# Three more attention units with V as the stationary operand of PV and key sums on Pool, and a later slot for the second norm

## The chip, the cores and the metric

The kernel runs on one core of a Trainium2 chip. A core has engines with instruction queues of their own: TensorE (PE) for matmuls, with a weight load (PEld) ahead of each; VectorE (DVE); ScalarE (ACT); GpSimd (POOL); and SyncE (SP), which here issues the DMA transfers. They wait for each other through semaphores. On-chip memory is SBUF; PE writes its results to banks of PSUM. The metric is the time of one execution in microseconds on the device, the median of the runs shown.

## The reference: what is computed

A transformer block on x of 2048 rows and 512 columns, in bf16. A modulation vector of six parts (sa, ca, ga, sb, cb, gb) is made from `c` and `w_mod`. Then

```python
h = layernorm(x) * (1 + ca) + sa
x = x + ga * attention(h)      # 32 query heads, 8 kv heads, head size 128, 2048 cached keys
h = layernorm(x) * (1 + cb) + sb
x = x + gb * gated_mlp(h)      # w_in, gelu, a 2048 x 2048 mixing matrix w_sp, w_out
```

Attention projects h with `wq`, takes softmax(q k^T / sqrt(128)) v for each head and projects with `wo`. Of the output of attention, four query heads share one kv head. The MLP normalises half of its hidden part and mixes it over the rows with `w_sp`.

## The kernel before

**Units.** Attention is cut into 128 units (`NU`). Unit u is kv group g = u // 16 (`HKV` = 8 groups) and query tile j = u % 16 of 128 rows (`NT` = 16), with the four query heads of that group (`REP`). A loop over iterations `it` from 0 to `NU + 5` starts the scores of unit `it`; each iteration has eight slots (`NSLOT`). In each slot the program writes, in this order: what was put off to that slot with `at(it, slot, fn)`; a part of the scores of unit `it` (`qk`, two or so 128 x 512 matmuls into a double bank of PSUM and one exp on ACT); a part of PV of an earlier unit (`pv_part`); a part of the q projection for later units (`fill`, L959); and one matmul of the output projection `wo` of a still earlier unit (L1209). The order on each engine is the order in which the program writes the instructions; nothing reorders them, so a waiting instruction holds up all behind it on its engine. PV of a unit comes one to three iterations after its scores (`pv_at`), its output projection three iterations after that (`wo_at`). PE's work in a steady iteration is 16 matmuls of scores, 16 or 64 of PV, 4 of `wo` and 4 of q.

**Three kinds of units.**
- *Row units* (`by_rows`; two of every three from unit 5 to 121, `TURN_A` to `TURN_B`) have queries on the partitions. The exp sums its row on the way (`accum_out`, L1033). The probabilities P are then transposed by a DMA that SP issues, one for each head (`turn_rows`, L1116), and DVE makes 1/sum from the row sums (L1120, L1123).
- *Sums units* (`by_sums`; every third one, 7, 10, ... up to 109) have keys on the partitions, so that P needs no transposing (L1063 for the scores, L1070 for the exp). Their row sums come from `key_sums`: Pool adds the 16 key tiles of P (15 adds, L1085), SP transposes the result (`xn<-onorm`, L1100), and two iterations and more later DVE reduces and inverts it (`close`, L1104, L1105).
- *Old column units* (the rest: 0 to 4, and 112, 115, 118 and 121 to 127) also have keys on the partitions, but take their sums from a column of ones beside V.

**PV.** Row and sums units use `pv_rows`: V is the stationary operand and P moves through, 16 matmuls of 512 columns (L1131) into one bank, whose result DVE casts to `oT` (L1140). The output projection then gets a bank for each head (`each` in `wo_proj`), and DVE scales each with 1/sum and adds it to `xacc` (L1202, four a unit). Old column units use `pv`: P is the stationary operand and V with the column of ones moves, 64 matmuls of 129 columns (L1152); DVE takes the reciprocal of the sums and scales (L1163, L1164, twice a unit), SP transposes (`oT<-onorm`, L1175), and the projection's four heads add up in one bank, which DVE adds to `xacc` once (L1196; in the first group it copies it, L1194).

**Where P lives.** The tile for a unit's P is one of three (`homes`: `pT0`, `pT1`, `wsp`), given out in turn as their last users are done. The transposes of a row unit therefore wait for all readers of the unit that had the tile before, and these are PV and, for a sums unit, Pool's adds.

**Start and end.** In the first iterations PE also waits for the first layernorm, in pieces: DVE normalises (L687), SP transposes, and DVE applies the modulation to the transposed tiles `hT` (L806, in `ln1_mod`), which the q projections read. In the last group (units 112 to 127) each output projection ends a query tile: x is updated (for tiles 0 to 11 by Pool, L1225 and L1226), and `ln2` does the second layernorm in three steps: `first` has the statistics on DVE (L698, L699) and 1/std on Pool (L679, L683); `second` normalises on DVE (L687) and has SP transpose the tile (`acc<-acc`, L1248); `third` applies the modulation on DVE (L1255). They are put in slots of the iterations after the projection. The MLP follows (L1436 to L1645), of which some is mixed into the last iterations. A fallback after it runs only if a softmax sum lies outside a safe range.

The slots of Pool's adds and of the second norm are set by these lines:

```python
for kt in range(1, NKT):
    at(*divmod(u * NSLOT + kt // 2 + 1, NSLOT), lambda kt=kt: add(kt))
...
at(it + 1, 0 if j >= NT - CT else 2, first)
at(it + 1, 4, second)
at(it + 2, 3, third)
```

`NKT` is 16 and `CT` is 4.

Of the kernel before, what the change touches and what calls it, by code (L numbers as in the profile page):

```python
# [575 lines left out]
def kernel(  # L576
# [21 lines left out]
    _, HKV, SK, DH = A_k_cache.shape  # L598
# [6 lines left out]
    NT = S // P  # L605
# [4 lines left out]
    CT = 512 // P  # L610
    FC = _f_chunk(FH)
    NFHC = FH // FC
    NSLOT = NKT // 2
# [62 lines left out]
    def rstd_of(mv, n, tag):  # L676

        ve = stat.tile([P, CT], FP32, name=f"ve_{tag}")
        nc.gpsimd.tensor_scalar(  # L679
            out=ve[:, :n], in0=mv[:, :, 1], scalar1=LN_EPS, scalar2=None, op0=ALU.add  # L680
        )
        rstd = stat.tile([P, CT], FP32, name=f"rstd_{tag}", bufs=4)
        nc.gpsimd.tensor_tensor(out=rstd[:, :n], in0=ve[:, :n], in1=mhalf[:, :n], op=ALU.pow)  # L683
        return rstd

    def normalise(dst, src, mv, rstd):
        nc.vector.tensor_scalar(  # L687
            out=dst,
            in0=src,
            scalar1=mv,  # L690
            scalar2=rstd,
            op0=ALU.subtract,
            op1=ALU.mult,
        )

    def ln_stats(mv, j, src):
        st = stat.tile([P, 1, nc.vector.BN_STATS_DIM], FP32, name="bnst")
        nc.vector.bn_stats(out=st[:, 0, :], in_=src)  # L698
        nc.vector.bn_aggr(out=mv[:, j, :], in_=st[:])  # L699
# [87 lines left out]
    def ln1_stats(j0, n):  # L787
        for j in range(j0, j0 + n):
            ln_stats(mv1, j, x_sb[:, j, :])
        return rstd_of(mv1[:, j0 : j0 + n, :], n, "ln1")  # L790
# [153 lines left out]
    first = {1: ln1_stats(1, 1)}  # L944
# [33 lines left out]
    TURN_A, TURN_B = CT + 1, NU - 6  # L978
# [3 lines left out]
    def by_rows(u):  # L982
        return TURN_A <= u < TURN_B and (u - TURN_A) % len(LAGS) < len(LAGS) - 1

    def by_sums(u):
        return TURN_A <= u < (HKV - 1) * NT and not by_rows(u)

    row_units = [u for u in range(NU) if by_rows(u)]

# [16 lines left out]
    def at(it, slot, fn):  # L1006
        later.setdefault((it, slot), []).append(fn)

    def qk(u, i):
        g, j = divmod(u, NT)  # L1010
        b, jj = g * NCH + j // CT, j % CT
        if i == 0:
            if homes[u] == "wsp":
                pTs[u] = wspp.tile([P, NT, 512], BF16, name="wsp")
            else:
                pTs[u] = late.tile([P, NKT, 512], BF16, name=homes[u], bufs=1)
            if by_rows(u):
                rsums[u] = stat.tile([P, NSLOT], FP32, name="rs")
            if by_sums(u):
                key_sums(u)  # L1020
# [56 lines left out]
    def key_sums(u):  # L1077
        acc = res.tile([P, D], FP32, name="acc", bufs=2)
        sums = late.tile([P, REP, DH], BF16, name="onorm", bufs=3)[:].rearrange(
            "p r q -> p (r q)"  # L1080
        )
        pT = pTs[u]

        def add(kt):
            nc.gpsimd.tensor_tensor(  # L1085
                out=acc[:] if kt < NKT - 1 else sums,
                in0=pT[:, 0, :] if kt == 1 else acc[:],
                in1=pT[:, kt, :],
                op=ALU.add,
            )  # L1090

        for kt in range(1, NKT):
            at(*divmod(u * NSLOT + kt // 2 + 1, NSLOT), lambda kt=kt: add(kt))

        turned = {}

        def turn():
            xn = res.tile([P, D], BF16, name="xn1", bufs=4)
            turned["t"] = xn[:].rearrange("p (r q) -> p r q", r=REP)
            nc.sync.dma_start_transpose(out=turned["t"], in_=sums)  # L1100

        def close():
            tot = stat.tile([P, REP], FP32, name="tot4")
            nc.vector.tensor_reduce(out=tot[:], in_=turned["t"], axis=AX.X, op=ALU.add)  # L1104
            nc.vector.reciprocal(out=rall[:, u * REP : (u + 1) * REP], in_=tot[:])  # L1105

        at(u + 2, 3, turn)
        at(u + 3, 2, close)
# [75 lines left out]
    def wo_proj(u):  # L1184
        g, j = divmod(u, NT)
        each = by_rows(u) or by_sums(u)
        ps = {}

# [45 lines left out]
    def ln2(it, j):  # L1234

        st = {}

        def first():
            if j < NT - CT:
                ln_stats(mv2, j, x_sb[:, j, :])  # L1240
            st["rstd"] = rstd_of(mv2[:, j : j + 1, :], 1, "ln2")

        def second():
            both = res.tile([P, D], FP32, name="acc", bufs=2)[:].bitcast(BF16)
            xn = both[:, 0:D]
            normalise(xn, x_sb[:, j, :], mv2[:, j, 0:1], st["rstd"][:, 0:1])
            st["xnT"] = both[:, D : 2 * D].rearrange("p (d q) -> p d q", d=NDT)
            nc.sync.dma_start_transpose(out=st["xnT"], in_=xn)  # L1248

        def third():  # L1250
            ch, c0 = j // CT, (j % CT) * P
            if ch not in h2Ts:
                h2Ts[ch] = res.tile([P, NDT, 512], BF16, name="hT", bufs=NCH)
            for dt in range(NDT):
                nc.vector.tensor_scalar(  # L1255
                    out=h2Ts[ch][:, dt, c0 : c0 + P],
                    in0=st["xnT"][:, dt, :],
                    scalar1=modc[:, 4 * NDT + dt : 4 * NDT + dt + 1],
                    scalar2=modc[:, 3 * NDT + dt : 3 * NDT + dt + 1],
                    op0=ALU.mult,  # L1260
                    op1=ALU.add,
                )

        at(it + 1, 0 if j >= NT - CT else 2, first)
        at(it + 1, 4, second)
        at(it + 2, 3, third)

    mod_b = {}
# [142 lines left out]
    for g in range(1, HKV):  # L1411
        it = (g - 1) * NT
# [100 lines left out]
    def pv_part(u, i, n):  # L1513
        if by_rows(u) or by_sums(u):
            return pv_rows(u, i, n)
        for k in range(NSLOT // n):
            pv(u, i * (NSLOT // n) + k)

    for it in range(NU + 6):
# [37 lines left out]
        for u in wos:  # L1557
            if u >= (HKV - 1) * NT:
                ln2(it, u % NT)
# [208 lines left out]
```

## Time and profile before

| what | value |
|---|---|
| median of three runs | 1297.49 us (1297.36 to 1297.56) |
| the profiled execution | 1297.41 us, its span 1295.6 us |
| busy PE / ACT / DVE / POOL | 1281.8 / 1109.0 / 775.1 / 665.2 us |
| matmuls of PV with V as weights (L1131) | 1157 and 563 recorded |
| matmuls of PV with P as weights (L1152) | 704 and 256 recorded |
| Pool's adds of the sums (L1085) | 234 and 221 in the two largest groups, 1156 ns each |

The profile is of one execution. Its parts: busy time of each engine; the span in 40 slices, a digit for the busy tenths of each; the chain of work that ended last, followed back from the end; and groups of instructions by line, with busy time, the mean of one, and the idle time of the engine ahead of them with what ended it. The timeline lists an engine's instructions one after the other: start, time, engine, line, operation, tiles, count, and in brackets the idle time before and what ended it. A window sums up one stretch. Times on these lists are microseconds from the start of the span, unless marked ns.

### The profile page before, as it was taken

How to read it: one execution, taken by the hardware profiler on the slowest of the kernel's cores; microseconds unless marked ns; L12 is line 12 of the kernel's file. 1: busy time of each engine (PE TensorE's matmuls, PEld its weight loads, DVE VectorE, ACT ScalarE, POOL GpSimd, SP SyncE). 2: the span in 40 equal slices, each digit the busy share in tenths (PEclk: the TensorE clock that was granted, in tenths of full speed). 3: DMA queues.
4: the chain of work that ended last, by engine and by line, in shares of the span. 5: the costliest groups of instructions: out<-in, count | busy, mean ns of one | idle time of the engine just before them, and what ended most of it. 6: DMA issues, size and time to landing. Idle time of an engine off the chain costs nothing.

```text
span 1295.6 us, 20137 instructions
## 1 busy us (share of the span) xinstructions
PE 1281.8 (99%) x6860; PEld 628.2 (48%) x6985; DVE 775.1 (60%) x1847; ACT 1109.0 (86%) x1683; POOL 665.2 (51%) x624
## 2 busy tenths in 40 slices
PE   9999999999999999999999999999999999999998
PEld 7644444444444444444444444444445556644445
DVE  7546656665666566656665666566656566784444
ACT  7999999999999999999999999999999998650000
POOL 2067756775677567756775677567750133410000
PEclk9999999999999999999999999999999999999999
DMA  7999999999999999999999999999999983264300
GB/s 207 187 194 175 169 191 185 190 171 189 186 191 171 193 161 195 188 177 188 184 184 176 187 188 187 168 193 173 186 196 162 165 150 88 51 141 99 78 21 32
DMA packets 774991, 211.02 MB, mean 163 GB/s; under 512 B 759264, under 2 KB 773216, under 8 KB 774880
## 3 DMA queue, kind: packets, MB, share of 16 engines
q1 hardware_dynamic: 772864, 207.94, 87.0%
q10 hardware_dynamic: 2016, 1.71, 0.4%
q8 instruction: 57, 0.93, 0.3%
q14 instruction: 54, 0.44, 0.1%
HBM read 21.37 MB, written 2.10 MB: 18 GB/s over the span
## 4 chain that ended last, share of the span: by engine, by line
PE 98%; issue 1%; ACT 1%; DMA 0%; SPq 0%; DVE 0%; ACTq 0%
PE o_ps L1131 30%; PE s_ps L1026 21%; PE s_ps L1063 13%; PE misc L1209 8%; PE misc L959 8%; PE misc L1612 7%; PE o_ps L1152 4%; PE s_ps L1436 2%; PE s_ps L1475 2%; PE o_ps L1645 1%; PE s_ps L1047 0%; ACT pn L1033 0%; PE s_ps L1645 0%; DMA kT<-in_A_k_cache_dram 0%; ACT pT L1054 0%
## 5 line engine op out<-in xcount | busy, mean ns | idle before, releaser
L1202 DVE SCALAR_TENSOR_TENSOR xacc<-misc,rall,xacc 128x512 f32<-128x512 f32 x441 | 330.3, 749 | 86.5 <-PE misc L1209 72.7
L1026 PE MATMUL s_ps<-kT,qT 128*128 128x512 bf16 x1243 | 370.1, 379 | 0.3
L1131 PE MATMUL o_ps<-pT,v 128*128 128x512 bf16 x1157 | 348.3, 379 | 3.1
L1033 ACT ACTIVATE win_sb<-s_ps 128x1024 bf16<-128x1024 f32 x312 | 318.9, 1023 | 3.4 <-PE s_ps L1026 0.7
L1131 PEld LDWEIGHTS <-v 128*128 128x128 bf16 x1808 | 176.9, 98 | 213.3
L1085 POOL TENSOR_TENSOR acc<-acc,wsp 128x512 f32<-128x512 f32 x234 | 270.5, 1156 | 18.3
L1085 POOL TENSOR_TENSOR acc<-acc,pT 128x512 f32<-128x512 f32 x221 | 255.5, 1156 | 17.3
L1063 PE MATMUL s_ps<-qT,kT 128*128 128x512 bf16 x768 | 228.4, 379 | 0.5
L1070 ACT ACTIVATE pT<-s_ps 128x1024 bf16<-128x1024 f32 x208 | 209.6, 1024 | 10.7 <-PE s_ps L1063 3.5
L1033 ACT ACTIVATE pn<-s_ps 128x1024 bf16<-128x1024 f32 x208 | 212.7, 1023 | 2.0 <-PE s_ps L1026 0.5
L1026 PEld LDWEIGHTS <-qT 128*128 128x128 bf16 x1248 | 121.5, 98 | 142.6 <-issue 0.7
L1209 PE MATMUL misc<-wo_g,oT 128*128 128x512 bf16 x500 | 189.5, 379 | 0.3
L1070 ACT ACTIVATE wsp<-s_ps 128x1024 bf16<-128x1024 f32 x176 | 179.7, 1023 | 11.2 <-PE s_ps L1063 4.2
L959 PE MATMUL misc<-hT,wq_g 128*128 128x512 bf16 (+1 forms) x523 | 187.4, 369 | 0.2
L970 DVE CAST qT<-misc 128x512 bf16<-128x512 f32 x126 | 86.9, 689 | 165.9 <-PE misc L959 165.9
L1131 PE MATMUL o_ps<-wsp,v 128*128 128x512 bf16 x563 | 169.8, 379 | 1.5
L1120 DVE TENSOR_REDUCE tot<-rs 128x1 f32<-128x2 f32 x312 | 46.1, 148 | 115.0 <-ACT win_sb L1033 76.3
L1063 PEld LDWEIGHTS <-kT 128*128 128x128 bf16 x768 | 74.0, 98 | 81.2 <-issue 1.1
L1033 ACT ACTIVATE wmod_a<-s_ps 128x1024 bf16<-128x1024 f32 x104 | 106.3, 1023 | 0.6 <-PE s_ps L1026 0.4
L1612 PE MATMUL misc<-wsp,z 128*128 128x512 bf16 (+2 forms) x554 | 100.1, 336 | 0.3
L1085 POOL TENSOR_TENSOR acc<-wsp 128x512 f32<-128x512 bf16 x18 | 20.7, 1151 | 149.9 <-ACT wsp L1070 149.9
L1140 DVE CAST oT<-o_ps 128x512 bf16<-128x512 f32 x113 | 78.2, 692 | 16.7 <-PE o_ps L1131 4.6
(127 smaller groups left out, 1004.7 us busy)
## 6 DMA issues: line engine op xcount, KB each, us to landing
wo_g<-in_A_wo_dram SPq DMA_DIRECT2D x8, 512.0 KB, 4.5
wq_g<-in_A_wq_dram SPq DMA_DIRECT2D x7, 512.0 KB, 4.3
v<-in_A_v_cache_dram SPq DMA_DIRECT2D x7, 512.0 KB, 4.7
wsp<-in_w_mod_dram SPq DMA_DIRECT2D x1, 2048.0 KB, 9.5
pT<-win_sb SPq DMA_TRANSPOSE x117, 4.7
win_sb<-in_B_w_in_dram SPq DMA_DIRECT2D x1, 1792.0 KB, 8.3
x_sb<-in_A_x_dram SPq DMA_DIRECT2D x3, 512.0 KB, 7.6
out_dram<-yout ACTq DMA_DIRECT2D x12, 128.0 KB, 1.7
```

The lines of the kernel that those rows point to most:

```text
L959: nc.tensor.matmul(ps[0][:, o0 : o0 + n], lhsT=wqs[g][:, dt, hh * DH : (hh + 1) * DH], rhs=hTs[ch][:, dt, c0 : c0 + n], start=(dt == 0), s ...
L970: nc.vector.tensor_copy(out=dst, in_=src)
L1026: nc.tensor.matmul(s_ps[:, c * 512 : (c + 1) * 512], lhsT=qTs[b][:, hh, jj * P : (jj + 1) * P], rhs=groups[g]["kT"][:, k0 : k0 + 512], sta ...
L1033: nc.scalar.activation(out=rows_of(u, hh)[:, half * HK : (half + 1) * HK], in_=s_ps[:], func=ACT.Exp, scale=inv_sqrt_dh, accum_out=rsums[u ...
L1063: nc.tensor.matmul(s_ps[:, h * 512 : (h + 1) * 512].rearrange("p (r q) -> p r q", r=REP), lhsT=groups[g]["kT"][:, kt * P : (kt + 1) * P], ...
L1070: nc.scalar.activation(out=pTs[u][:, 2 * i : 2 * i + 2, :], in_=s_ps[:].rearrange("p (k q) -> p k q", k=2), func=ACT.Exp, scale=inv_sqrt_dh,)
L1085: nc.gpsimd.tensor_tensor(out=acc[:] if kt < NKT - 1 else sums, in0=pT[:, 0, :] if kt == 1 else acc[:], in1=pT[:, kt, :], op=ALU.add,)
L1131: nc.tensor.matmul(o_pss[u][:], lhsT=groups[g]["v1"][:, kt, 0:DH], rhs=pTs[u][:, kt, :], start=(kt == 0), stop=(kt == NKT - 1),)
L1140: nc.vector.tensor_copy(out=oTs[u][:], in_=o_pss[u][:].rearrange("p (r q) -> p r q", r=REP))
L1202: nc.vector.scalar_tensor_tensor(out=xa[:], in0=X_ps[:], scalar=scale, in1=xa[:], op0=ALU.mult, op1=ALU.add)
L1209: nc.tensor.matmul(ps[0][:], lhsT=oTs[u][:, hh, :], rhs=groups[g]["wo"][:, hh, :], start=(hh == 0 or each), stop=(hh == REP - 1 or each),)
L1612: nc.tensor.matmul(g_pss[f][:, :n], lhsT=z2[:, st, f * P : (f + 1) * P], rhs=wsp[t][:, st, c0 : c0 + n], start=(st == 0), stop=(st == NT - ...
```

## The change

Three edits. `by_sums` takes in unit 4 (the last one ahead of the row units) and units 112 and 115 (the first two old column units of the last group), so these three use `pv_rows`, `key_sums` and a bank for each head in the projection; 118 and 121 to 127 stay as they were. For units from 112 on the adds of the sums are `paced`: add number kt goes to slot 1 + 8 (kt - 1) // 7 after the unit's start instead of 1 + kt // 2, which spreads the 15 adds over some two iterations instead of one. And for query tiles 0 to 11 the first and second step of `ln2` go from slots 2 and 4 to slots 3 and 5; the third stays.

```diff
     def by_sums(u):
-        return TURN_A <= u < (HKV - 1) * NT and not by_rows(u)
+        return TURN_A - 1 <= u <= (HKV - 1) * NT + 3 and not by_rows(u)
 ...
+        paced = u >= (HKV - 1) * NT
         for kt in range(1, NKT):
-            at(*divmod(u * NSLOT + kt // 2 + 1, NSLOT), lambda kt=kt: add(kt))
+            slot = 1 + (8 * (kt - 1)) // 7 if paced else 1 + kt // 2
+            at(*divmod(u * NSLOT + slot, NSLOT), lambda kt=kt: add(kt))
 ...
-        at(it + 1, 0 if j >= NT - CT else 2, first)
-        at(it + 1, 4, second)
+        at(it + 1, 0 if j >= NT - CT else 3, first)
+        at(it + 1, 4 if j >= NT - CT else 5, second)
         at(it + 2, 3, third)
```

Lines below the second edit have numbers higher by two in the changed kernel (L1131 becomes L1133).

## The prediction

> **What bounds the kernel now.** I read the busy shares and the chain first, then the groups of instructions, then the single iterations that the change touches, window by window.
>
> ```profile
> PE 1281.8 (99%) x6860; PEld 628.2 (48%) x6985; DVE 775.1 (60%) x1847; ACT 1109.0 (86%) x1683; POOL 665.2 (51%) x624
> POOL 2067756775677567756775677567750133410000
> PE 98%; issue 1%; ACT 1%; DMA 0%; SPq 0%; DVE 0%; ACTq 0%
> ```
>
> TensorE is busy for 99% of the span and is 98% of the chain; its clock row is full throughout. So a microsecond counts only if it leaves the PE stream or makes PE wait. The Pool row is empty in its second slice (32 to 65 us) and in its 31st (972 to 1004), the two places where the new units put their adds.
>
> ```profile
> L1085 POOL TENSOR_TENSOR acc<-acc,wsp 128x512 f32<-128x512 f32 x234 | 270.5, 1156 | 18.3
> L1140 DVE CAST oT<-o_ps 128x512 bf16<-128x512 f32 x113 | 78.2, 692 | 16.7 <-PE o_ps L1131 4.6
> L1152 PE MATMUL o_ps<-v,pT 128*128 128x129 bf16 x704 | 53.6, 220 | 0.1
> ```
>
> The 220 and 379 ns that these groups give for one matmul include its drain, so the pitch has to come from start to start:
>
> ```profile
> 1005.40 0.59 PE L1131 MATMUL o_ps<-pT,v 128*128 128x512 bf16 x2
> 1005.83 0.59 PE L1063 MATMUL s_ps<-qT,kT 128*128 128x512 bf16 x2
> ...
> 1015.03 0.62 PE L1152 MATMUL o_ps<-v,wsp 128*128 128x129 bf16 x8
> 1015.48 0.38 PE L1209 MATMUL misc<-wo_g,oT 128*128 128x512 bf16 x1
> ```
>
> Two 512-wide matmuls take 0.43 us to the next start, 0.216 each; eight 129-wide ones 0.45, 0.056 each. The same holds in whole iterations (columns: length, then busy time and count of PE, PEld, DVE, ACT, POOL, then clock, DMA share, GB/s):
>
> ```profile
> 999.14:1007.77 8.63, 8.58 (x40) 3.91 (x40) 4.64 (x9) 8.13 (x10) 0.00 (x0) 1.00 1.11 208
> 1007.77:1016.58 8.81, 8.76 (x88) 5.98 (x88) 3.52 (x12) 8.42 (x16) 0.00 (x0) 1.00 0.71 83
> 981.46:990.26 8.80, 8.75 (x88) 5.97 (x88) 5.66 (x15) 8.41 (x16) 0.00 (x0) 1.00 0.58 109
> 49.70:58.08 8.38, 8.28 (x86) 5.78 (x87) 4.12 (x16) 8.30 (x16) 0.00 (x0) 1.00 0.82 147
> ```
>
> The first has the new kind of PV, the other three the old PV of units 115, 112 and 4. PE fills each to 0.05 to 0.10 us.
>
> **The change part by part.** *PV on PE.* Each of the three units loses 64 matmuls of 0.0564, 3.61 us, and gets 16 of 0.216, 3.45: 0.16. The windows say 8.81 against 8.63, 0.18. I take 0.17 and three times that, 0.5 us. Nearest bounds: nothing for unit 4, where ACT is busy 8.30 of 8.38 and may hold the iteration up (gain 0.35 in all), and 0.6.
>
> Here the Trainium skill (TensorE: Matmul & The Clock Gate, Back-to-back issue gap) speaks for much more: it has streams with weight loads at about 81 ns for each 128-wide and 131 ns for each 512-wide matmul. By it a unit would gain 64 x 81 - 16 x 131 = 3.1 us, 9.3 in all, an estimate; the 56 and 216 ns above contradict both figures.
>
> *DVE.* A converted unit loses two reciprocals (0.17) and two scalings (0.42) and one add of the projection (0.69): 1.9 us. It gets a cast (0.69), a reduction (0.67), a reciprocal (0.18) and four scaled adds (0.75 each): 4.5. That is 2.7 us more, spread over four iterations in which DVE is busy 3.5 to 5.7 of 8.8 us. Its cover is that idle time; without it PE would wait for a bank, up to 2.7 us a unit. In steady iterations the same work leaves PE at 8.58 of 8.63, so I cost it at nothing.
>
> *Pool.* 15 adds of 1.156 us at a pitch of 1.23 make 18.4 us a unit. Pool is idle from 44.6 to 68.4 us, and from 965.7 to 1016.7, so the sums of 4, 112 and 115 end at about 63, 993 and 1022 (the last with the pair of L1225 and L1226, 2.4 us, among them; the paced slots leave them only two adds behind them). They hold what reads them, the next user of that P tile: the transposes of units 6, 114 and 117. The first of these went out at 64.50, the last at 1023.60, both after the sums' end. So nothing; if the adds ran late, the nearest PV deadline behind such a transpose has 1.2 to 1.7 us to spare (landing 997.91 for a start at 999.14, 1023.57 for 1025.27).
>
> *SP.* Three transposes of normalised outputs (L1175) go, three of sums (L1100) come; a slot of 1.2 to 1.3 us of the queue either way. What they feed is wanted an iteration later (the reduction of L1104, then L1202): estimated landing 68.4 and close at 68.6 for unit 4, 1027.8 and 1027.5 for unit 115, where DVE has 1.6 us idle before its next work. Nothing.
>
> *ln2 a slot later, units 112 to 123.* Its first and second part move past one row transpose on SP. That transpose took 1.2 to 2.8 us of the queue, so `acc<-acc` (L1248) lands up to that much later, while the row head that it no longer precedes goes out 1.3 us earlier. Who waits is the third part on DVE, and behind it the cast of q:
>
> ```profile
> 1057.16 0.98 DVE L1255 TENSOR_SCALAR hT<-acc,modc 128x128 bf16<-128x128 bf16 x4 [1.15 <-DMA acc<-acc]
> 1058.06 0.68 DVE L970 CAST qT<-misc 128x512 bf16<-128x512 f32 x1
> ```
>
> DVE waited 1.15 us there already; the PE matmul that needs the cast's bank starts at 1058.95, 0.2 after it. Here lateness would reach PE one to one. Ends: a loss of 1.9 us (2.1 later, less 0.2) if the transpose ahead is slow, a gain of 0.2 if the heads that go out earlier shorten the backlog. In the other iterations DVE has idle time before the third part and I estimate 1 us of lateness against 1.4 of slack. I take 0.1, near the lower end, because in most of the twelve the row shows no wait at all.
>
> *Reductions at L698* that now wait for Pool's x_sb (0.40 to 1.0 us each of DVE) lose that wait. PE did not wait behind it: nothing.
>
> *Sum.* Profiled run 1297.41, of which 1295.6 is the span and 1.8 lies around it; the median shown is 1297.49, 0.08 above. 1297.49 - 0.5 + 0.1 = 1297.1.
>
> **The rivals.** *A: Pool's adds of unit 4 block DVE (slower).* From 44.6 to 63 they run beside DVE work that today has an idle Pool next to it:
>
> ```profile
> 44.59 1.39 DVE L687 TENSOR_SCALAR xn<-x_sb,mv,rstd_ln 128x512 bf16<-128x512 bf16 x4 [0.97 <-POOL rstd_ln L683]
> 46.43 1.37 DVE L806 TENSOR_SCALAR hT<-hT,modc 128x512 bf16<-128x512 bf16 x4
> 54.96 1.38 DVE L806 TENSOR_SCALAR hT<-hT,modc 128x512 bf16<-128x512 bf16 x4
> 50.23 0.68 DVE L1194 COPY xacc<-misc 128x512 f32<-128x512 f32 x1
> ```
>
> The first three are 0.35 us each, SBUF to SBUF in bf16, and no such operation meets an add anywhere in this trace. Operations that read PSUM meet adds all the time and are no slower (L1202 0.75, L1140 0.69). The nearest row for the others is one Pool multiply at 1103.75 that took 1.36 beside an L687, 0.09 above the group's 1.27. If each of the twelve operations waits for one add of 1.156, a group ends 4.6 us later: L687 at 50.6 instead of 46.0, the first L806 at 52.1, where a q matmul at 50.59 reads it. PE loses 1.5 us there; followed on, 1.8 at the projection near 56 (its bank is freed by L1194 behind them), and 2.4 at the q matmul near 63: 5.7, giving 1302.7. If only the first of each four waits (1.2), nothing reaches PE. It decides from the second wait in a group. The 0.09 speaks for little, but it is one instruction and Pool's, not DVE's.
>
> The rule for this is in the Trainium skill (SBUF — State Buffer, Who interferes with whom): a tensor_scalar in its two-port mode and a GpSimd operation exclude each other for the whole instruction, whoever issues first. It doesn't say who goes next when both queue; no run here shows it yet.
>
> *B: SP's order starves DVE's third part.* Lateness at the iterations with no slack (118, 121) of 0.2 to 1.9 us: 1297.3 to 1298.9. Against it: a row head leaves earlier by as much, and the tightest one (landed 1050.97 for a PV at 1051.40) becomes safer.
>
> *C: the saving does not show.* If ACT paces these iterations (8.41 and 8.42 of 8.80 and 8.81), PE's gain turns into idle time: 1297.5. The new-kind window has ACT at 8.13, which speaks against.
>
> *D: the PE pitch shrinks as in the skill's rule above.* 1288; the two pitches in the trace all but exclude it.
>
> **How the numbers follow.** About 0.2%, 2.6 us, is what a measurement of this kernel can tell from no change. The forecast with its small waits has 0.38, C 0.07, both within that. A has 0.34: 0.28 for two or more stalls, above 1300.1, and 0.06 for one of 1.5 to 2. B has 0.17: 0.10 for the times given there, 0.07 that the lateness carries over from iteration to iteration and passes 1300.1. D has 0.01, and 0.03 go to earlier row heads taking away several waits that I read as noise; both are faster. So faster 0.01 + 0.03 = 0.04, same 0.38 + 0.07 + 0.06 + 0.10 = 0.61, slower 0.28 + 0.07 = 0.35. The range goes from 1296.5 (all of the gain, 0.6, and 0.4 of waits gone) to 1302.8 (A in full); the likeliest case's own is 1296.5 to 1298.9.
>
> **What would show it.** PE with 288 matmuls and their loads fewer and its busy time down by 0.5; iterations 113 and 116 (L1131 with unit 112's and 115's P) of 8.63 instead of 8.80; L1085 with 45 more at 1.156; DVE up by 8 us. For A: the L687 and L806 groups near 45 and 55 us, 1.4 us long or 2.5 or 6; PE gaps before q matmuls from 50 to 64. For B: the wait of L1255 for `acc<-acc` in iterations 118 to 125, and PE idle behind it. I am wrong if PE's busy time in a new PV is not that of the old kind less 0.17, or if any DVE group near 45 us grows past 3 us.

## The result, and the profile after

The changed kernel takes 1300.18 us (median of 14 runs, 1299.82 to 1300.63), the kernel before 1297.58 (14 runs, 1297.36 to 1298.11). The ratio is 1.0020, 95% interval 1.0011 to 1.0028: 2.6 us slower, where 0.4 us faster was forecast. The profiled execution took 1299.82 us; its span, 1298.0, is 2.4 longer than that of before.

The page of the changed kernel, busy shares and chain:

```profile
PE 1282.0 (99%) x6718; PEld 622.0 (48%) x6841; DVE 794.3 (61%) x1853; ACT 1109.7 (85%) x1683; POOL 718.2 (55%) x669
PE 96%; DVE 2%; issue 1%; DMA 1%; SPq 0%; ACT 0%; POOL 0%; DVEq 0%
```

PE has 142 fewer matmuls recorded (144 were taken out, with as many weight loads), Pool 45 more. New is DVE with 2% of the chain, where it had 0%. The waits of PE (line, what it waited for, us in total, times, longest) tell which work that is:

```profile
PE misc L959 <- DVE xacc L1196: 1.2, 1, 1.2
PE misc L1211 <- DVE tot L1122: 0.8, 1, 0.8
...
PE misc L1211 <- DVE qT L970: 0.3, 1, 0.3
```

None of these three was there before. The first two lie at 62.08 and 55.60 us, the third at 1061.24. Here is DVE's timeline of the changed kernel around the first two, the same groups that the prediction showed for before:

```profile
44.54 4.94 DVE L687 TENSOR_SCALAR xn<-x_sb,mv,rstd_ln 128x512 bf16<-128x512 bf16 x4 [0.97 <-POOL rstd_ln L683]
49.93 4.48 DVE L806 TENSOR_SCALAR hT<-hT,modc 128x512 bf16<-128x512 bf16 x4
54.87 0.68 DVE L1196 COPY xacc<-misc 128x512 f32<-128x512 f32 x1
56.08 4.50 DVE L806 TENSOR_SCALAR hT<-hT,modc 128x512 bf16<-128x512 bf16 x4
61.35 0.68 DVE L1196 COPY xacc<-misc 128x512 f32<-128x512 f32 x1
```

And Pool beside them:

```profile
44.48 1.15 POOL L1085 TENSOR_TENSOR acc<-pT 128x512 f32<-128x512 bf16 x1
45.71 15.95 POOL L1085 TENSOR_TENSOR acc<-acc,pT 128x512 f32<-128x512 f32 x13
61.74 1.16 POOL L1085 TENSOR_TENSOR onorm<-acc,pT 128x512 bf16<-128x512 f32 x1
```

Groups of four that took 1.39, 1.37 and 1.38 us take 4.94, 4.48 and 4.50 while Pool adds. The copies L1196, which read PSUM, still take 0.68, but come late behind the groups, and with them the banks that PE waits for. (The row of the second wait names the reduction L1122, which PE does not use. The copy ahead of it ended at 55.55, 0.05 before the matmul starts; in e10, the same kernel again, the list names the copy for this wait and the reduction for the other.) One more stall is too short for this list: the q matmul at 50.77 starts 0.47 us after the matmul ahead of it, where 0.22 is usual, 0.05 after the first operation of the L806 group has ended.

To see where the time went over the whole run I took the first exp of each unit in ACT's timeline and the distance to the first exp of the next as the length of an iteration. The table has the profiled executions of both kernels and of those below that matter here (us):

| kernel | 5 and 6 together | 113 | 114 and 115 | 116 | 118 | 121 |
|---|---|---|---|---|---|---|
| before | 16.96 | 8.94 | 17.37 | 8.94 | 8.48 | 8.48 |
| the change | 19.31 | 8.84 | 17.17 | 8.84 | 8.48 | 8.90 |
| e1, unit 4 alone | 19.30 | 8.94 | 17.18 | 8.94 | 8.48 | 8.48 |
| e7, unit 4, half adds | 16.79 | 8.94 | 17.18 | 8.94 | 8.48 | 8.49 |
| e5, shift alone | 16.96 | 8.95 | 17.37 | 8.95 | 8.68 | 10.52 |
| e14, the change with half adds | 16.78 | 8.84 | 17.17 | 8.84 | 8.48 | 9.60 |

All other iterations come out equal (7 to 112 in sum). So the change lost 2.35 us in iterations 5 and 6, gained 0.10 in 113 and in 116 and 0.20 in 114 and 115, and lost 0.42 in 121: +2.37, against 2.34 from span to span (the first exp came 0.05 earlier).

### The profile page after: what moved, and what is told of

Same layout as the page of the kernel before. It is cut to its first block, busy times and chain, and to the rows that moved or that the text cites. A ratio compares the mean times of both kernels' runs of the same rounds, so it can differ in the third digit from the quotient of the medians.

```text
span 1298.0 us, 19923 instructions
## 1 busy us (share of the span) xinstructions
PE 1282.0 (99%) x6718; PEld 622.0 (48%) x6841; DVE 794.3 (61%) x1853; ACT 1109.7 (85%) x1683; POOL 718.2 (55%) x669
## 3 DMA queue, kind: packets, MB, share of 16 engines
q10 hardware_dynamic: 2016, 1.71, 0.4%
## 4 chain that ended last, share of the span: by engine, by line
PE 96%; DVE 2%; issue 1%; DMA 1%; SPq 0%; ACT 0%; POOL 0%; DVEq 0%
PE o_ps L1133 30%; PE s_ps L1026 20%; PE s_ps L1063 12%; PE misc L1211 8%; PE misc L959 8%; PE misc L1614 7%; PE o_ps L1154 3%; PE s_ps L1438 2%; PE s_ps L1477 2%; PE o_ps L1647 1%; DVE hT L806 1%; PE s_ps L1047 0%; DVE xn L687 0%; PE s_ps L1647 0%; DMA kT<-in_A_k_cache_dram 0%
## 5 line engine op out<-in xcount | busy, mean ns | idle before, releaser
L1204 DVE SCALAR_TENSOR_TENSOR xacc<-misc,rall,xacc 128x512 f32<-128x512 f32 x452 | 338.3, 748 | 90.0 <-PE misc L1211 76.1
L1133 PE MATMUL o_ps<-pT,v 128*128 128x512 bf16 x1187 | 357.5, 379 | 3.2
L1085 POOL TENSOR_TENSOR acc<-acc,pT 128x512 f32<-128x512 f32 x247 | 285.8, 1157 | 19.8 <-ACT pT L1070 0.5
L1085 POOL TENSOR_TENSOR acc<-acc,wsp 128x512 f32<-128x512 f32 x247 | 285.9, 1157 | 19.3
L1133 PEld LDWEIGHTS <-v 128*128 128x128 bf16 x1856 | 181.6, 98 | 219.0 <-issue 0.2
L1133 PE MATMUL o_ps<-wsp,v 128*128 128x512 bf16 x579 | 174.6, 379 | 1.6
L1122 DVE TENSOR_REDUCE tot<-rs 128x1 f32<-128x2 f32 x312 | 46.3, 148 | 108.7 <-ACT win_sb L1033 73.0
L1085 POOL TENSOR_TENSOR acc<-pT 128x512 f32<-128x512 bf16 x19 | 22.0, 1155 | 133.1 <-ACT pT L1070 133.1
```

What stands on the lines that cost most here:

```text
L1085: nc.gpsimd.tensor_tensor(out=acc[:] if kt < NKT - 1 else sums, in0=pT[:, 0, :] if kt == 1 else acc[:], in1=pT[:, kt, :], op=ALU.add,)
L1122: nc.vector.tensor_reduce(out=tot[:], in_=rs[:, 2 * hh : 2 * hh + 2], axis=AX.X, op=ALU.add)
L1133: nc.tensor.matmul(o_pss[u][:], lhsT=groups[g]["v1"][:, kt, 0:DH], rhs=pTs[u][:, kt, :], start=(kt == 0), stop=(kt == NKT - 1),)
L1204: nc.vector.scalar_tensor_tensor(out=xa[:], in0=X_ps[:], scalar=scale, in1=xa[:], op0=ALU.mult, op1=ALU.add)
```

## The experiments

Times are medians; "before" is the kernel before on the same chip.

### Unit 4 alone, and the change without it

e1 takes only this part of the change:

```diff
-        return TURN_A <= u < (HKV - 1) * NT and not by_rows(u)
+        return TURN_A - 1 <= u < (HKV - 1) * NT and not by_rows(u)
```

> Only unit 4 becomes a sums unit; units 112 and 115, the paced adds and the slots of the second norm stay as before. Theory (Pool's adds and DVE's two-port work take turns): the L687 group near 45 us takes 4.9 us and the two L806 groups 4.5 each, PE loses about 2.4 and gains 0.1 to 0.2, so 2.2 to 2.6 us slower than before (about 1299.9). Rival (the loss lies in the last group): within 0.3 us of before.

1299.90 against 1297.67, ratio 1.0018 (1.0009 to 1.0028). Iterations 5 and 6 take 19.30 together as in the change. As the theory had it; on its own that doesn't say whether the adds or the conversion did it.

e2 is the change with `TURN_A` in place of `TURN_A - 1`.

> The change without unit 4. Theory: iterations 113 and 116 gain 0.1 each, iteration 121 loses 0.4 because the statistics of the norm now stand between the third step and the q cast on DVE: 0.1 to 0.3 us slower than before (about 1297.8), with L687 and L806 groups near 45 us of 1.4 us. Rival (the loss is in the tail): 1.5 us or more slower.

1299.88 against 1297.67, ratio 1.0017 (1.0008 to 1.0027), in a wide spread (1298.49 to 1300.78). I had expected some 1297.8: this was the rival's time. Iterations 113 and 116 gain 0.11 and 0.10, but iteration 121 takes 9.45 in the profiled execution, which at 1298.49 was the shortest; nine of the other ten took 1.3 to 2.3 us more, and no profile shows where. So 2.2 us for unit 4 and 2.2 for the rest, and yet 2.6 for both: the parts do not add up, which set the later runs.

### The adds without the conversion

e4 leaves unit 4 as it was and adds only Pool work that nothing waits for:

```diff
+    def idle_adds(u):
+        acc = res.tile([P, D], FP32, name="acc", bufs=2)
+        def add(kt):
+            nc.gpsimd.tensor_tensor(
+                out=acc[:],
+                in0=x_sb[:, 0, :] if kt == 1 else acc[:],
+                in1=x_sb[:, 0, :],
+                op=ALU.add,
+            )
+        for kt in range(1, NKT):
+            at(*divmod(u * NSLOT + kt // 2 + 1, NSLOT), lambda kt=kt: add(kt))
...
+            if u == TURN_A - 1:
+                idle_adds(u)
```

> The kernel before with 15 more Pool adds of 128x512 in the slots of unit 4's, on a scratch tile and a tile of x that nothing waits for; their result is not used. Unit 4 keeps its old PV. Theory: the adds alone stretch the L687 and L806 groups to 4.5 to 5 us and cost PE the same 2.3 to 2.7 us (about 1300.1). Rival (the conversion does it: the DVE operations added, the banks taken one by one, the P tile held by the adds): within 0.2 us of before.

1299.97 against 1297.67, ratio 1.0018 (1.0009 to 1.0027). DVE's timeline of e4:

```profile
44.80 4.83 DVE L687 TENSOR_SCALAR xn<-x_sb,mv,rstd_ln 128x512 bf16<-128x512 bf16 x4 [0.97 <-POOL rstd_ln L683]
50.08 4.48 DVE L806 TENSOR_SCALAR hT<-hT,modc 128x512 bf16<-128x512 bf16 x4
56.76 4.04 DVE L806 TENSOR_SCALAR hT<-hT,modc 128x512 bf16<-128x512 bf16 x4
```

The whole loss is there with nothing converted. It is Pool's adds, running beside these DVE operations, that cost the time.

### The same adds in halves

e7 is e1 with each of unit 4's adds cut in two:

```diff
+            cuts = (0, 256, 512) if u < TURN_A else (0, 512)
+            for a, b in zip(cuts, cuts[1:]):
                 nc.gpsimd.tensor_tensor(
-                    out=acc[:] if kt < NKT - 1 else sums,
+                    out=acc[:, a:b] if kt < NKT - 1 else sums[:, a:b],
...
```

> Only unit 4 converted, each of its Pool adds cut into two of 256 columns. Theory (a two-port DVE operation gets one turn for each Pool add): the turn comes after half the time, so the L687 and L806 groups take some 2.6 us instead of 4.5 to 4.9, and PE loses 0 to 0.7 instead of 2.3: 1297.6 to 1298.3. Rival (Pool's total time at the port counts): groups of 4.5 to 5 us and 1299.9 as with whole adds.

1297.38 against 1297.78, ratio 0.9996 (0.9987 to 1.0005); 2.5 us less than with whole adds. DVE and then Pool in e7:

```profile
44.95 2.79 DVE L687 TENSOR_SCALAR xn<-x_sb,mv,rstd_ln 128x512 bf16<-128x512 bf16 x4 [0.97 <-POOL rstd_ln L683]
48.19 2.88 DVE L806 TENSOR_SCALAR hT<-hT,modc 128x512 bf16<-128x512 bf16 x4
55.29 2.88 DVE L806 TENSOR_SCALAR hT<-hT,modc 128x512 bf16<-128x512 bf16 x4
```

```profile
46.19 16.90 POOL L1087 TENSOR_TENSOR acc<-acc,pT 128x256 f32<-128x256 f32 x26
```

One half add has a pitch of 16.90 / 26 = 0.65 us, and one DVE operation of these groups now takes 0.70 to 0.72. With whole adds the pitch is 15.95 / 13 = 1.23 and one DVE operation takes 4.94 / 4 = 1.24 in the first group, 1.12 in the others. So each operation gets about one turn for each Pool add, at both sizes. The groups still end 1.4 to 1.5 later than alone, and PE waits for none of it. Iterations 5 and 6 are 0.17 shorter than before: the gain of the shorter PV, which the stall had hidden.

### The same adds, held back

e12 converts unit 4 and makes Pool wait for DVE instead: a small Pool operation reads the last tile of each L806 group (`hold`), five adds run between the two groups and ten after the second.

```diff
+        def hold(ch):
+            mark = stat.tile([P, 1], FP32, name="mark")
+            nc.gpsimd.tensor_scalar(
+                out=mark[:], in0=hTs[ch][:, 3, 0:1], scalar1=0.0, scalar2=None, op0=ALU.add
+            )
+        if u < TURN_A:
+            at(u, 5, lambda: hold(2))
+            at(u + 1, 5, lambda: hold(3))
         for kt in range(1, NKT):
+            slot = kt // 2 + 1 if u >= TURN_A else 6 + kt if kt <= 5 else 14 + (kt - 6) // 2
...
-        at(u + 3, 2, close)
+        at(u + 3, 2 if u >= TURN_A else 7, close)
```

> Only unit 4 converted; its adds wait until the L806 groups are through: the first five run between the groups of slots (4,5) and (5,5), the rest after the second, each part behind a small Pool operation that reads hT; the closing step of its sums comes five slots later. Theory: the three groups are back at 1.4 us and PE gets the gain of the shorter PV: 0 to 0.2 us faster than before. Rival (the conversion itself, or the P tile held 5 us longer, costs PE): 0.5 us or more slower.

1302.08 against 1297.78, ratio 1.0030 (1.0020 to 1.0040). DVE, and then the first waiting matmul of PE, in e12:

```profile
44.87 1.38 DVE L687 TENSOR_SCALAR xn<-x_sb,mv,rstd_ln 128x512 bf16<-128x512 bf16 x4 [0.97 <-POOL rstd_ln L683]
46.70 1.38 DVE L806 TENSOR_SCALAR hT<-hT,modc 128x512 bf16<-128x512 bf16 x4
55.22 1.38 DVE L806 TENSOR_SCALAR hT<-hT,modc 128x512 bf16<-128x512 bf16 x4
```

```profile
95.55 0.59 PE L1141 MATMUL o_ps<-pT,v 128*128 128x512 bf16 x2 [2.94 <-issue]
```

Apart in time from the adds, the groups are back at 1.38 us, and iterations 5 and 6 take 16.78. But the forecast was wrong, and the rival's second half fits: the adds end at 69.1 instead of 63, the transposes of unit 6 that reuse the P tile start at 69.15, each one behind it follows later, and the last of the four heads that a PV needs lands at 95.46, 0.1 before that PV starts after 2.9 us of waiting. The row names no releaser, so this is read from the times. The profiled execution (1300.50) is one of the three short ones; the other six took 1.5 us or more longer, and what they lost besides is not shown. So what has to be left alone is DVE in these 20 us and, by this reading, the P tile after 63.

### The slot of the second norm

e3 is e2 with the norm's steps back in slots 2 and 4.

> Units 112 and 115 with paced adds, the second norm in its old slots 2 and 4. Theory: without the slot shift the 0.4 us of iteration 121 go and 0.2 are gained, 0.1 to 0.3 us faster than before (about 1297.4). Rival (the shift is needed, since Pool's update of x comes late among the adds of unit 115): DVE waits at the statistics in iteration 117, PE loses 0.5 to 2 us there, 1298 or more.

1297.75 against 1297.67, ratio 1.0001 (0.9992 to 1.0010): 2.1 us less than with the shift. The predicted 0.2 of gain doesn't show in the medians (iterations 113 and 116 take 8.84, but 121 takes 8.68); the shift was not needed for units 112 and 115. What the 0.20 in iteration 121 is, I do not know. e5 is the shift alone, on the kernel before:

```diff
-        at(it + 1, 0 if j >= NT - CT else 2, first)
-        at(it + 1, 4, second)
+        at(it + 1, 0 if j >= NT - CT else 3, first)
+        at(it + 1, 4 if j >= NT - CT else 5, second)
```

> The kernel before with the second norm's first and second step a slot later, nothing else. Theory (the shift costs the tail: the transpose of the norm lands later and the statistics come to stand behind the waiting third step, so the q cast of iteration 121 is late): slower by 0.8 to 2.3 us (1298.5 to 1300). Rival (the two converted units cost it, the shift is free): within 0.3 us of before.

1299.88 against 1297.73, ratio 1.0016 (1.0007 to 1.0025). The shift costs all of e2's loss without any new unit, 2.04 of it in iteration 121. The statistics of the kernel before, then DVE there in e5, and after it in the change itself:

```profile
1054.04 0.69 DVE L698 BATCH_NORM_STATS2 bnst<-x_sb 128x6 f32<-128x512 bf16 x1 [0.40 <-POOL x_sb L1226]
```

```profile
1058.84 0.98 DVE L1255 TENSOR_SCALAR hT<-acc,modc 128x128 bf16<-128x128 bf16 x4 [2.55 <-DMA acc<-acc]
1059.74 0.68 DVE L698 BATCH_NORM_STATS2 bnst<-x_sb 128x6 f32<-128x512 bf16 x1
...
1060.55 0.66 DVE L970 CAST qT<-misc 128x512 bf16<-128x512 f32 x1
```

```profile
1058.82 0.98 DVE L1257 TENSOR_SCALAR hT<-acc,modc 128x128 bf16<-128x128 bf16 x4 [0.93 <-DMA acc<-acc]
1059.71 0.69 DVE L698 BATCH_NORM_STATS2 bnst<-x_sb 128x6 f32<-128x512 bf16 x1
...
1060.53 0.66 DVE L970 CAST qT<-misc 128x512 bf16<-128x512 f32 x1
```

In the kernel before the cast followed the third step at once, 0.90 after its start; the statistics had been done 3 us earlier, ahead of the wait. Now they stand between the two, and the cast starts 1.71 after the third step. So the shift does two things: the third step waits for a transpose that is issued later, and in iteration 121 the cast behind it is 0.8 later still. e8 is e2 with only the first step put back (slot 2); the second stays in slot 5:

> Units 112 and 115 converted, the second step of the norm in slot 5, its first step back in slot 2. Theory (two parts: the late transpose and the statistics behind the third step): the 0.8 us of statistics leave the way to the cast, the late transpose stays: between the 1299.9 with both shifted and the 1297.75 with none, some 1298.5 to 1299.2. Rival (only the late transpose counts): as with both, 1299.9.

1299.24 against 1297.73, ratio 1.0009 (1.0000 to 1.0018), spread from 1297.67 to 1299.79. The median lies between e2 and e3, as the theory with two parts has it, but its place is another: in the profiled execution (1299.79, the longest) iteration 121 loses only 0.16, and iteration 118, where no statistics stand ahead of the cast in any of these kernels, loses 1.95, because the norm's transpose lands 4.31 after its issue, with a transfer of instructions under way from 1031.01 (more on these below). e9 is e2, with both steps shifted, but with the third step of query tiles 0 to 7 out of the cast's way:

```diff
-        at(it + 2, 3, third)
+        at(it + 2, 3 if j >= 2 * CT else 5, third)
```

> Units 112 and 115 converted, both steps shifted, and the third step of query tiles 0 to 7 in slot 5 instead of 3, so that the q cast no longer queues behind its wait. Theory (PE waits only for the cast behind the third step): the loss goes, 1297.3 to 1297.8. Rival (the loss comes from row transposes or P tiles that are late): stays at 1299 or more.

1297.47 against 1297.73, ratio 0.9997 (0.9988 to 1.0006). Iterations 118 and 121 take 8.48 as before, although the transpose of 118 lands as late in the iteration as in e8 (6.99 after the first exp). With this the cast no longer waits, and the loss of e2 is gone.

### Why the parts do not add up

e10 is the change again, to have it on the same chip as e5:

> The change itself, unaltered, on the same chip as the parts. If the parts add up (2.2 for unit 4, 2.2 for the shift): 1302. If it stays at 1300.2, as first measured, the stall at unit 4 takes away most of what the shift costs later, and the profile has iteration 121 some 0.4 longer and not 1 to 2.

1300.62 against 1297.73, ratio 1.0021 (1.0012 to 1.0030), with 121 at 8.98 and 118 at 8.88. So the shift costs 0.4 to 0.9 in the change and 2.0 to 2.2 alone. The traces point at one thing first. The DMA view of e5 from 1056 to 1059 us (40 slices of 0.075 us), and of the change from 1057.6 to 1060.6, the same place within its iteration:

```profile
GB/s 82 198 222 461 208 208 218 181 85 11 0 0 0 0 0 0 7 7 10 7 10 10 7 10 10 10 21 7 0 0 20 65 191 188 208 225 205 201 201 225
...
q8 instruction: 1, 0.02, 2.0%
```

```profile
GB/s 133 222 215 225 191 239 191 201 79 14 0 0 0 0 0 0 10 99 195 212 232 198 232 215 212 205 205 205 215 215 198 229 212 229 205 225 212 229 208 225
...
q1 hardware_dynamic: 1945, 0.49, 84.0%
```

In e5 a 16 KB transfer of instructions (queue q8, at 1056.28) falls into the stretch and almost nothing else moves for some 1.5 us: the norm's transpose lands 4.03 after its issue, in the change, with no such transfer there, 2.44 (a gap of half a microsecond is in its view too). This is not one chance meeting. In the kernel before, 36 such transfers start between 100 and 1060 us; from 0.7 to 1.6 us after their start all other queues together moved 19 GB/s on the mean, and under 40 in 33 of the 36, against 181 over the whole stretch. One of them, at 1055.12, meets the norm's transpose of iteration 121 as well, which lands 5.29 after its issue. There it costs nothing, because without the shift the transpose is issued 2.6 us earlier in the iteration. If the transfer falls by the number of instructions ahead of it, a converted unit moves it: that has 48 matmuls and 48 weight loads fewer. Two runs move it with more and narrower warm-up matmuls at the start of the kernel. e11 does so to e5, with 52 of 96 columns, e13 to the change, with 35 of 144 (shown):

```diff
-    warm(10)
+    w_ps = bank("o_ps")
+    for k in range(35):
+        nc.tensor.matmul(
+            w_ps[:, 0:144],
+            lhsT=zeros[:, 0, :],
+            rhs=zeros[:].rearrange("p r d -> p (r d)")[:, 0:144],
...
```

> The shift of the second norm alone, as before, with the ten warm-up matmuls of 512 columns at the start replaced by 52 of 96: 84 more PE instructions, 0.1 to 0.3 us of time at the start either way. Theory (the 16 KB transfer of instructions at 1056.28 held up the transposes for 1.5 to 2 us and met the iteration without slack): that transfer now comes some 9 us earlier, outside 1050 to 1058, and iteration 121 loses 0.3 to 1.0 instead of 2.0: 1298 to 1299. Rival (the shift costs the 2 us by itself): 1299.9 as without it.

> The whole change, with the ten warm-up matmuls replaced by 35 of 144 columns: 50 more PE instructions. Theory: the transfer of instructions that came at 1061.87, after the critical transpose, now comes 4 to 6 us earlier and meets it: iteration 121 loses 1.5 to 2 more, 1301.5 to 1302.2. Rival (position of that transfer is of no account): 1300.2 to 1300.6 as before.

e11 took 1301.54 against 1297.78, ratio 1.0028 (1.0018 to 1.0039): a miss. The new start costs 1.9 us by unit 3's first exp (35.14 against 33.12, less the 0.10 of the first), not 0.1 to 0.3; without that it would still be 1299.6, above the forecast. Iteration 121 came down from 10.52 to 9.92 only, and 118 rose from 8.68 to 9.14; the transfer had moved from 1056.3 to 1050.2. e13 took 1302.03, ratio 1.0032 (1.0020 to 1.0044), in the forecast range, but by luck: 0.8 of it is the start, and without that it would be 1301.2, under the range. What counts is iteration 121: 10.09 instead of 8.90 and 8.98. The DMA view of e13 from 1057 to 1061 us:

```profile
GB/s 220 220 218 220 212 230 225 212 374 212 195 205 110 28 5 0 0 0 8 8 10 10 8 10 10 46 274 289 257 287 292 287 292 106 0 26 146 205 197 223
...
q8 instruction: 1, 0.02, 1.5%
```

The 50 instructions more brought the transfer from 7.8 to 2.6 us after the iteration's first exp, into the time in which the critical transpose is under way, and 1.1 us more are lost there. The rival idea was that the stall at unit 4 gave the transposes time which they used up later. e14 removes the stall and leaves the number of PE instructions: the change with e7's half adds.

> The whole change, unit 4's adds cut into halves of 256 columns, so that the stall near 45 to 62 us goes. It tells apart why the shift cost 2.2 us without unit 4 and 0.4 to 0.9 with it. Theory F (the transfer of instructions is placed by the number of PE instructions, which is that of the change): it comes some 8 us after the start of iteration 121, behind the critical transpose, iteration 121 loses 0.4 to 0.5, and the time is 1297.5 to 1298. Theory R (the early stall of 2.4 us gave the transposes time that they use up later): without the stall the shift costs its 2.2 and the time is 1299.4 to 1299.9.

1297.94 against 1297.70, ratio 1.0003 (0.9994 to 1.0012). That is theory F's time, and 2 us from theory R's. It is not the whole of it: in its profiled execution (1298.38) no such transfer lies between 1038 and 1060 us, and iteration 121 still takes 9.60, not theory F's 8.9 to 9.0, since the norm's transpose is issued 0.7 later in the iteration than in the change (1054.81 with the iteration's first exp at 1051.88, against 1056.35 with 1054.11).

What the loss follows can be read off the executions themselves. The table has times after the first exp of the iteration, and by how much the iteration is longer than 8.48 (us):

| kernel, iteration | transpose issued | issue to landing | q cast starts | longer by |
|---|---|---|---|---|
| before, 121 | -0.38 | 5.29 | 5.83 | 0.00 |
| the change, 121 | 2.25 | 2.44 | 6.43 | 0.42 |
| e10 (the change), 118 | 2.99 | 2.47 | 6.37 | 0.40 |
| e2, 121 | 2.38 | 2.86 | 6.98 | 0.97 |
| e5, 121 | 2.27 | 4.03 | 8.05 | 2.04 |
| e8, 118 | 2.70 | 4.31 | 7.93 | 1.95 |
| e8, 121 | 2.41 | 2.81 | 6.15 | 0.16 |
| e11, 121 | 3.24 | 2.46 | 7.44 | 1.44 |
| e13, 121 | 2.23 | 3.65 | 7.61 | 1.61 |
| e14, 121 | 2.93 | 2.45 | 7.12 | 1.12 |

In every row with a loss, the loss is the time by which the cast starts later than 6.0 (5.97 to 6.01). Three things set that start: when SP issues the transpose, how long it takes to land (3.65 or more in the four rows with a transfer of instructions under way, 2.9 or less in the others), and in iteration 121 the statistics. The landing time makes the difference between e5 and the change. The stall at unit 4 does not set the issue, which is the same in e5, without the stall, as in the change. Why SP issues 0.7 to 1.0 later in e14 and e11 is not shown.

### What is left when both costs go

e15 is e14 with e9's third step; e16 is e14 with the norm back in its old slots.

> As before, with the third step of query tiles 0 to 7 in slot 5 as well. Both costs found are removed and the shorter PV stays: 0.3 to 0.5 us faster than the kernel before (1297.1 to 1297.4). If a loss at iterations 118 or 121 stays, the third step was not what made PE wait.

> All three units converted, unit 4's adds in halves, the second norm in its old slots. 0.2 to 0.5 us faster than before (1297.1 to 1297.5) if the shift was not needed for units 112 and 115; 1298 or more if Pool's late update of x then holds DVE in iteration 117.

e15: 1297.15 against 1297.70, ratio 0.9997 (0.9988 to 1.0006). e16: 1297.12, ratio 0.9995 (0.9986 to 1.0004), 11 runs from 1296.94 to 1297.24, all below the lowest of 27 of the kernel before, 1297.33, though the interval of the ratio still holds 1. In both PE waits for nothing on DVE in the two places, and iterations 118 and 121 take 8.48. So the three units are worth about half a microsecond, of which 0.2 is the unexplained gain of iterations 114 and 115, and the change's 2.6 us are the two costs less this.

## Why the prediction was wrong

**PV on PE** held in kind and was a little large. 0.17 a unit was right for unit 4 (16.96 to 16.79 in e7); for 112 and 115 it is 0.10. At the end of these iterations PE comes to the next scores 0.06 late (0.49 us after the two matmuls of 1017.97, in place of 0.43), which I take for a wait on ACT, whose read of the exp's sum ends 0.05 before, but did not test. So 0.37 in place of 0.5. The Trainium skill's figures for a stream with weight loads (TensorE: Matmul & The Clock Gate, Back-to-back issue gap), which would have made it 9.3, are not what these windows show. The 0.20 of iterations 114 and 115 also comes whenever unit 4 is converted (e1, e7): one exp of iteration 114 then starts 4.6 us after the first instead of 4.9. I have no cause for it.

**DVE and Pool, "so nothing".** This is the step that failed. I looked for who reads the sums and whether Pool was idle, and put what idle Pool meant for DVE into rival A, with 0.34, not into the sum. Measured, this term is 2.53 us. Rival A named the operations and the way: each L687 and L806 waits for an add, and its sign, a group past 3 us near 45, came. Its sizes were too large. I let each operation wait a whole add and then run, 1.16 + 0.35; it took one pitch of the adds, 1.12 to 1.24, so the groups grew by 3.1 to 3.6 us and not by 4.6. And of its three stalls the first, at the q matmul of 50.59, was 0.25 and not 1.5: this matmul had to wait only for the first of the four operations, which ended at 50.71. The other two came at the projection (0.95 against 1.8) and at the q matmul near 62 (1.33 against 2.4), both for banks that the late copies L1196 free. (These are from start to start; the list of waits counts from the modelled end of the matmul ahead, and has 0.8 and 1.2.) Together 2.53 in place of 5.7; less the 0.17 of the shorter PV that is the 2.35 of iterations 5 and 6. With all terms as measured, -0.37 - 0.20 + 2.53 + 0.42 is 2.38, where the table has 2.37. The bound "from the second wait in a group" was right: in e7 the same waits, half as long, reach nothing.

The Trainium skill's rule (SBUF — State Buffer, Who interferes with whom) agrees in who is hit: SBUF to SBUF tensor_scalar, and not the copies, casts and scaled adds that read PSUM. That one side blocks for the whole instruction of the other fits DVE's rows; on Pool's side 13 adds take 15.95 beside the DVE groups and took 15.96 without them, so Pool lost nothing. The second figure is from the kernel before:

```profile
949.64 15.96 POOL L1085 TENSOR_TENSOR acc<-acc,wsp 128x512 f32<-128x512 f32 x13
```

**ln2, "I take 0.1".** The iteration (121) and the victim (the q cast, and the PE matmul behind it) were right, and the upper end of 1.9 was near what the shift costs alone (2.1). In the change itself it is 0.4 to 0.9, and there the way was another in iteration 121: the third step L1255 does not start later than before but 0.2 earlier (4.71 against 4.93 us after the first exp). The failed part is one line: that the statistics L698 lose a wait and cost nothing. I followed what they no longer wait for, and not what they are now queued behind: a slot later they come after the waiting third step and ahead of the cast, 0.8 us on the way to PE. Less the 0.2 and the 0.2 of slack that I had read, that is the 0.42. That the transposes can also meet a transfer of instructions was in none of the cases.

**SP and Pool's end times** held: no PV was late for its P tile in the change. In e12 the adds ended 6 us later, and a PV waited 2.9.

**The chances.** 0.61 lay on "within 0.2%" and 0.35 on slower; the measured 0.20% lies on the border between them, on the other side of the forecast's sign.

## What to carry to other kernels

Before work is put on an idle engine, list what the other engines do in that stretch that has never run beside it: an operation that the trace only shows alone has no price yet. If the work must go there, cut its instructions small; the neighbour waits one instruction at a time. When a step is moved by a slot on an in-order engine, read what now stands between a waiting instruction and the next one that PE needs.

## What the runs showed of the hardware

A DVE tensor_scalar of 128x512 bf16 from SBUF to SBUF takes 0.35 us alone, 1.0 to 1.24 beside Pool adds of 512 columns (the change, e4) and 0.70 to 0.72 beside adds of 256 (e7): about one turn for each Pool instruction. Pool's pitch does not change (15.95 us for 13 adds, 15.96 without such operations).

A 16 KB transfer of instructions (q8) went with 1.1 to 1.5 us in which the DMA transposes all but stood still, at 0 to 21 GB/s instead of some 210 (e13, e5); in the kernel before, 33 of 36 such transfers are followed by a stretch of 0.9 us under 40 GB/s. Its place follows the number of PE instructions ahead of it: 84 more at the start brought it 8.5 us earlier in iteration 121 (e11), 50 more 5.2 (e13). So an edit at the start of a kernel can move a loss of 1 us at the end of it.
